# Attention steps in three parts, and column scales applied in the third stage's splits

## The chip, the cores and the metric

The kernel runs on one core of a Trainium2 chip. The metric is the time of one execution in microseconds of the device; the median of three runs is given. TensorE (PE) multiplies, VectorE (DVE) and ScalarE (ACT) do the work between, GpSimd (POOL) very little, and SyncE (SP) issues nearly all DMAs through one queue.

## The reference

```
q_n, k_n = rmsnorm(q, g_q), rmsnorm(k, g_k)            # 4 x 12 heads, 448 x 64
attn = softmax(q_n @ k_n.T / sqrt(64))
x = (attn @ v) laid out as 1792 x 768                  # 4 batches of 448 rows
x = ((x @ w_a) * (x @ w_b)) @ w_out                    # 768 -> 1536 -> 768
h = x @ w_in                                           # 768 -> 2048
g = max(h, 0) + alpha * min(h, 0)                      # alpha: one per column of h
out = g @ w2_out                                       # 2048 -> 768
```

The four weight matrices come as 64-bit floats (the kernel reads them as pairs of 32-bit words), everything else as 32-bit floats.

## The kernel before

The kernel works batch by batch (four batches, b = 0 to 3) and keeps every activation transposed, features on partitions and the 448 rows of the batch along the free dimension. Four stages follow attention for each batch: **a** (the product of the two first matmuls, 24 units of weights of 128 columns), **y** (12 units, two per block of 128 columns), **h** (16 units, with the leaky part behind it) and **o** (24 units, four per block of columns). The order of the stages is written out in the list `stages`: a0 y0 h0 o0 a1 y1 a2 h1 o1 y2 a3 h2 y3 o2 h3 o3.

Each operand of these matmuls is split into two 16-bit halves (a high half by ScalarE, `x[:, 0]`, the rest by VectorE, `x[:, 1]`), and `prod` makes three matmuls of 128x448 of each pair. To stay within 16 bits, weights and activations are scaled by powers of two. For weights the scale is one per column of the result: `w_convert` unpacks a 64-bit unit into 32 bits (ScalarE line 631, VectorE lines 634 and 637) and sums its squares (line 653); `w_scale` adds them over partitions with a small matmul (`total`, names `tot` and `tots`) and makes the scale `sc` and its inverse, kept in `inv`; `w_split` makes the two halves (lines 686 and 687) and stores them in a scratch in HBM, from which the later batches load them. Units are loaded 10, converted 8, summed 6 and split 3 units ahead of their use (`STEPS`). Only the first batch's stages (a0, y0, h0, o0) convert weights.

The inverse scales of stages a, y and o are applied when the result leaves PSUM. Those of stage h are not: the converted weights of stage o are multiplied by them, row block by row block (line 643, `inv["h"]`). Stage h itself takes each result out of PSUM in two steps (`t`, lines 832 and 833) and splits it with one scale `cg` for all blocks into `G[b, f]`. `slot` and `slot32` take tiles from a pool of 35 that all these operands share. In stage o, `finish` scales a result (line 847), transposes it on TensorE (line 854), multiplies it by the product of all scales left, `cum` (line 856, VectorE), and writes it out.

Attention goes in steps. A step m covers two blocks of 128 queries: `scores(m + 1)` on TensorE, `soft(m)` (maximum on VectorE, exponentials `pf` on ScalarE), `probs(m - 1)` (division, two 16-bit halves `p16`, DMA transposes into `pT`), then preparations for later pairs of heads (`prep0` squares, `prep1` inverse roots, `prep2` to `prep4` scaling, halves and transposes of q and k; `vnorm`, `vscale`, `vprep2` for v), and for a finished pair `pv` and `pv_out`, which makes a block of x. The first batch's attention runs alone at the start. The steps of the later batches are put between the units of the stages by `RATE`: 14 steps over the 24 units of a1, for instance. All of this is one program order; a scheduler then sets the final order on each engine, and each engine works through its own in order.

Of the kernel before, what the change touches and what calls it, by code (L numbers as in the profile page):

```python
# [19 lines left out]
def attention_gated_mlps_kernel(  # L20
# [73 lines left out]
    icg = const.tile([128, 1], F32, name="icg")  # L94
    ssv = const.tile([KP, B, NP], F32, name="ssv")
# [365 lines left out]
    def probs(m):  # L461
        if 2 * m < NP * NI:
            probs_f(m)
            return
# [4 lines left out]
        for j in range(2):  # L469
# [13 lines left out]
            )  # L483

# [44 lines left out]
    state = dict(pin=True)  # L529
# [3 lines left out]
    def att_steps():  # L533
# [3 lines left out]
        for m in range(total + 3):  # L537
            if m + 1 < total:
                scores(m + 1)
            if m < total:  # L540
                soft(m)
            if 1 <= m <= total:
                probs(m - 1)
            fin = None
            for n in range(2 * m + 2 if m else 0, 2 * m + 4):
                g, c = divmod(n, NI)
                if n < 2 * total:
                    if g >= NP:
                        if c == 0 and g % NP == 0:
                            vscale(g // NP)  # L550
                        if c == 2:
                            vprep2(g)
                        if c == 3:
                            load_v(g + 2)
                    ahead = (g + 1, g + 2) if g % 2 else ()
                    if c == 0:
                        for x in ahead:
# [13 lines left out]
                    if c == 6 and g + NP < B * NP:  # L571
# [49 lines left out]
    def w_convert(u):  # L621
# [18 lines left out]
        if kind == "o":  # L640
            k = CHAINS["o"][2]
            t3 = t.rearrange("p (k f) -> p k f", f=128)
            nc.vector.tensor_tensor(  # L643
                t3, t3,
                inv["h"][:, part * k:(part + 1) * k].unsqueeze(2).to_broadcast([128, k, 128]),
                op=ALU.mult,
            )
# [13 lines left out]
    def w_scale(u):  # L661
# [10 lines left out]
        for x in us:  # L672
            scales[x] = sc[:, (x - us[0]) // parts:(x - us[0]) // parts + 1]

# [115 lines left out]
    def stage_y(b):  # L790
# [21 lines left out]
        c = cum[:, b:b + 1]  # L812
        nc.gpsimd.tensor_tensor(c, ix[:, b:b + 1], iab[:, b:b + 1], op=ALU.mult)
        nc.gpsimd.tensor_tensor(c, c, iy[:, b:b + 1], op=ALU.mult)
        nc.gpsimd.tensor_tensor(c, c, icg, op=ALU.mult)
        nc.gpsimd.tensor_tensor(c, c, ix[:, b:b + 1], op=ALU.mult)
# [6 lines left out]
    def stage_h(b):  # L823
        for f in range(KF2):
# [6 lines left out]
            t = tmp()  # L831
# [4 lines left out]
            G[b, f] = split(t, cg, f"g{b}_{f}")  # L836
# [3 lines left out]
    def stage_o(b):  # L840
# [3 lines left out]
        def finish(m, ps):  # L844
# [11 lines left out]
            nc.vector.tensor_scalar(ob, po, cum[:PT, b:b + 1], None, op0=ALU.mult)  # L856
# [4 lines left out]

        late = None
# [21 lines left out]
    if True:  # L884
# [20 lines left out]
        while done < NP:  # L905
            g = next(att)
# [15 lines left out]
        for i, st in enumerate(stages):  # L922
# [7 lines left out]
            want, acc = RATE.get(st, 0), 0  # L930
# [35 lines left out]
```

## Time and profile before

| what | value |
|---|---|
| median of 3 runs (lowest, highest) | 1284.11 us (1283.06, 1289.75) |
| profiled execution: time, span | 1286.1 us, 1283.9 us |
| TensorE matmuls, busy | 1177.9 us, 92% |
| VectorE, busy | 709.6 us, 55% |
| ScalarE, busy | 734.5 us, 57% |
| stages a0 to y1 of the page's span | 117.65 to 653.60 us |

The busy share is one over the whole span; the program has a first half in which weights are converted and attention is dense, and a second in which both are thin, so the stretches have to be read one by one. Matmuls are pipelined, and a stretch in which TensorE is always busy runs at full speed only if the granted clock is 1.00 too.

### The profile page before, as it was taken

How to read it: one execution, taken by the hardware profiler on the slowest of the kernel's cores; microseconds unless marked ns; L12 is line 12 of the kernel's file. 1: busy time of each engine (PE TensorE's matmuls, PEld its weight loads, DVE VectorE, ACT ScalarE, POOL GpSimd, SP SyncE). 2: the span in 40 equal slices, each digit the busy share in tenths (PEclk: the TensorE clock that was granted, in tenths of full speed). 3: DMA queues.
4: the chain of work that ended last, by engine and by line, in shares of the span. 5: the costliest groups of instructions: out<-in, count | busy, mean ns of one | idle time of the engine just before them, and what ended most of it. 6: DMA issues, size and time to landing. Idle time of an engine off the chain costs nothing. (4 is left out here: it accounts for less than half of the span.)

```text
span 1283.9 us, 18197 instructions
## 1 busy us (share of the span) xinstructions
PE 1177.9 (92%) x6574; PEld 604.0 (47%) x6574; DVE 709.6 (55%) x1500; ACT 734.5 (57%) x1480; POOL 9.8 (1%) x32
## 2 busy tenths in 40 slices
PE   6897998888888889887999989999999999999998
PEld 3454544444443444443545545555555555555554
DVE  7988788879897857576545166443111351102410
ACT  7999898999886867577554256544222342212310
POOL 1000000000000000000000000000000000000000
PEclk9998998898998999997999999999999999999999
DMA  6548999999989899986865375687533333344343
GB/s 187 157 156 195 299 295 299 268 296 269 285 220 251 238 235 226 206 210 164 204 153 152 115 169 133 153 189 179 150 112 113 121 112 119 94 137 137 104 124 86
DMA packets 324489, 234.66 MB, mean 183 GB/s; under 512 B 190992, under 2 KB 297744, under 8 KB 324400
## 3 DMA queue, kind: packets, MB, share of 16 engines
q1 hardware_dynamic: 324288, 233.43, 68.9%
q8 instruction: 52, 0.85, 0.3%
q0 software_dynamic: 112, 0.07, 0.1%
q14 instruction: 37, 0.30, 0.1%
HBM read 155.79 MB, written 32.24 MB: 146 GB/s over the span
## 5 line engine op out<-in xcount | busy, mean ns | idle before, releaser
L108 PEld LDWEIGHTS <-w 128*128 128x128 f16 x4896 | 480.2, 100 | 488.8 <-issue 55.5
L108 PE MATMUL p<-x,w 128*128 128x448 f16 x1728 | 339.7, 356 | 10.1 <-ACT t L760 6.7
L108 PE MATMUL p<-g,w 128*128 128x448 f16 x1152 | 232.9, 359 | 9.9 <-DVE w L687 6.9
L108 PE MATMUL p<-y,w 128*128 128x448 f16 x1152 | 225.2, 357 | 0.0
L108 PE MATMUL p<-ab,w 128*128 128x448 f16 x864 | 170.8, 359 | 1.9 <-ACT ab L741 1.9
L108 PE MATMUL s<-kT,qT 128*64 128x448 f16 (+1 forms) x588 | 105.5, 408 | 32.4 <-ACT pf L431 24.7
L414 DVE TENSOR_REDUCE nm<-s 128x2 f32<-128x896 f32 x84 | 91.0, 1084 | 36.2 <-PE s L108 35.9
L475 DVE SCALAR_TENSOR_TENSOR p<-pf,ri,p 128x448 f16<-128x448 f32 x126 | 83.2, 680 | 37.9 <-ACT p L474 37.9
L474 ACT ACTIVATE p<-pf,ri 128x448 f16<-128x448 f32 x126 | 79.9, 662 | 31.9 <-DMA pT<-p 23.5
L431 ACT ACTIVATE pf<-s,nm,esc 128x448 f32<-128x448 f32 x126 | 90.2, 720 | 2.9 <-DVE p L475 1.5
L763 DVE SCALAR_TENSOR_TENSOR ab<-p,inv_a,t 128x448 f32<-128x448 f32 x48 | 32.6, 679 | 100.2 <-PE p L108 99.8
L847 ACT ACTIVATE t<-p,inv_o 128x448 f32<-128x448 f32 x24 | 25.6, 1066 | 102.2 <-PE p L108 102.2
L631 ACT ACTIVATE wf<-raw 128x768 f32<-128x768 f32 (+1 forms) x76 | 63.2, 835 | 28.7 <-DMA raw<-in_moe_w_out_dram 8.8
L856 DVE TENSOR_SCALAR ob<-p,cum 112x512 f32<-112x512 f32 x24 | 18.0, 749 | 107.1 <-PE p L854 56.8
L687 DVE SCALAR_TENSOR_TENSOR w<-wf,sc,w 128x768 f16<-128x768 f32 (+1 forms) x76 | 69.8, 927 | 4.0 <-ACT w L686 3.7
L766 ACT ACTIVATE junk<-ab 128x448 bf16<-128x448 f32 x48 | 27.5, 573 | 74.9 <-DVE ab L763 74.1
L833 DVE SCALAR_TENSOR_TENSOR t<-t,al,p 128x448 f32<-128x448 f32 x64 | 43.4, 679 | 47.6 <-ACT t L832 47.6
L637 DVE SCALAR_TENSOR_TENSOR wf<-raw,wf 128x768 int32<-128x768 int32 (+1 forms) x76 | 65.8, 868 | 0.4
L832 ACT ACTIVATE t<-p 128x448 f32<-128x448 f32 x64 | 34.6, 541 | 54.3 <-PE p L108 54.1
L686 ACT ACTIVATE w<-wf,sc 128x768 f16<-128x768 f32 (+1 forms) x76 | 64.5, 862 | 0.3 <-DVE sc L118 0.3
L653 ACT ACTIVATE junk<-wf 128x768 bf16<-128x768 f32 (+1 forms) x76 | 59.0, 776 | 8.5 <-DVE wf L643 2.9
L741 ACT ACTIVATE g<-t,cg 128x448 f16<-128x448 f32 x64 | 42.6, 666 | 34.7 <-DVE t L833 34.6
(131 smaller groups left out, 1003.3 us busy)
## 6 DMA issues: line engine op xcount, KB each, us to landing
w<-sc_a SPq DMA_DIRECT2D x72, 384.0 KB, 3.2
w<-sc_h SPq DMA_DIRECT2D x48, 384.0 KB, 3.1
w<-sc_o SPq DMA_DIRECT2D x72, 256.0 KB, 3.1
w<-sc_y SPq DMA_DIRECT2D x36, 384.0 KB, 3.2
raw<-in_moe_w_in_dram SPq DMA_DIRECT2D x16, 768.0 KB, 7.0
raw<-in_moe_w_out_dram SPq DMA_DIRECT2D x24, 512.0 KB, 5.0
raw<-in_moe_w_a_dram SPq DMA_DIRECT2D x12, 768.0 KB, 7.2
raw<-in_moe_w_b_dram SPq DMA_DIRECT2D x12, 768.0 KB, 6.0
```

The source lines that it names most:

```text
L108: nc.tensor.matmul(out=o, lhsT=a, rhs=b, start=first, stop=last)
L414: nc.vector.tensor_reduce(out=nm, in_=ps[:, :, 0:S], axis=AX.X, op=ALU.max, negate=True)
L431: nc.scalar.activation(out=pf, in_=ps[:, j, 0:S], func=AF.Exp, bias=nm[:, j:j + 1], scale=scale[j], accum_out=su[:, j:j + 1],)
L474: nc.scalar.activation(out=t[:, 0, :, 0:KP], in_=pf, func=AF.Copy, scale=r)
L475: nc.vector.scalar_tensor_tensor(out=t[:, 1, :, 0:KP], in0=pf, scalar=r, in1=t[:, 0, :, 0:KP], op0=ALU.mult, op1=ALU.subtract,)
L631: nc.scalar.activation(out=t, in_=hi.bitcast(F32), func=AF.Prelu, scale=2.0 ** -112, alpha=-(2.0 ** 32))
L637: nc.vector.scalar_tensor_tensor(out=ti, in0=lo, scalar=29, in1=ti, op0=ALU.logical_shift_right, op1=ALU.bitwise_or)
L653: nc.scalar.activation(out=junk(768, size(kind)), in_=t, func=AF.Square, accum_out=sums[0][:, j:j + 1])
L686: nc.scalar.activation(out=w[:, 0], in_=t, func=AF.Copy, scale=s)
L687: nc.vector.scalar_tensor_tensor(out=w[:, 1], in0=t, scalar=s, in1=w[:, 0], op0=ALU.mult, op1=ALU.subtract)
L741: nc.scalar.activation(out=x[:, 0], in_=t, func=AF.Copy, scale=s)
L833: nc.vector.scalar_tensor_tensor(out=t, in0=t, scalar=al[:, f:f + 1], in1=ps, op0=ALU.mult, op1=ALU.add)
```

## The change

Three things are done. Attention steps become three parts each, a `yield` after `soft` and one between the two blocks of `probs`, and the rates count thirds; a few preparations move to other places of a pair. The inverse column scales of stage h are no longer multiplied into stage o's weights; they go, divided by their largest, into the scale with which stage h's results are split (`cgf`, one column per block), and the largest goes into `icg` and with it into `cum`. In the first batch the scales are complete only during stage h, so its early blocks wait as 32-bit tiles until `h_scales` has run. And the output's last scaling moves from VectorE to ScalarE.

```
@@ probs, att_steps
             nc.sync.dma_start_transpose(
                 out=P[g]["pT"][:, :, c, :], in_=t.rearrange("p l i j -> p (l i j)")
             )
+            if j == 0:
+                yield
...
             if m < total:
                 soft(m)
+            yield None
             if 1 <= m <= total:
-                probs(m - 1)
+                for _ in probs(m - 1):
+                    yield None
+            else:
+                yield None
...
-                        if c == 2:
+                        if c == 5:
                             vprep2(g)
-                        if c == 3:
+                        if c == 6:
                             load_v(g + 2)
                     ahead = (g + 1, g + 2) if g % 2 else ()
+                    if g > 1 and g % 2 == 0 and c == 6:
+                        prep0(g + 2)
                     if c == 0:
-                        for x in ahead:
+                        for x in ahead[1 if g > 1 else 0:]:
                             prep0(x)
...
-                    if c == 6 and g + NP < B * NP:
+                    if c == (6 if g % 2 or g < NP else 1) and g + NP < B * NP:
                         vnorm(g // NP + 1, g % NP)
@@ w_convert, w_scale
-        if kind == "o":
-            k = CHAINS["o"][2]
-            t3 = t.rearrange("p (k f) -> p k f", f=128)
-            nc.vector.tensor_tensor(
-                t3, t3,
-                inv["h"][:, part * k:(part + 1) * k].unsqueeze(2).to_broadcast([128, k, 128]),
-                op=ALU.mult,
-            )
...
+        if (kind, n) == ("h", KF2 - 1):
+            h_scales()
+
+    def h_scales():
+
+        mx = sm_p.tile([128, 1], F32, tag="mh", name="mh")
+        ci = sm_p.tile([128, 1], F32, tag="mh", name="ci")
+        nc.vector.tensor_reduce(out=mx, in_=inv["h"], axis=AX.X, op=ALU.max)
+        nc.vector.tensor_scalar(
+            ci.bitcast(I32), mx.bitcast(I32), -1.0, float(254 << 23), op0=ALU.mult, op1=ALU.add
+        )
+        nc.vector.tensor_scalar(cgf, inv["h"], ci, cg, op0=ALU.mult, op1=ALU.mult)
+        nc.gpsimd.tensor_tensor(icg, icg, mx, op=ALU.mult)
+        state["cgf"] = True
@@ stage_h
+        def one(f):
+            t = raw.pop(f)
+            G[b, f] = x = slot(f"g{b}_{f}")
+            nc.scalar.activation(out=x[:, 0], in_=t, func=AF.Copy, scale=cgf[:, f:f + 1])
+            nc.vector.scalar_tensor_tensor(
+                out=x[:, 1], in0=t, scalar=cgf[:, f:f + 1], in1=x[:, 0],
+                op0=ALU.mult, op1=ALU.subtract,
+            )
...
-            t = tmp()
+            raw[f] = t = tmp() if state["cgf"] else slot32(f"g32_{b}_{f}")
...
-            G[b, f] = split(t, cg, f"g{b}_{f}")
+            if state["cgf"]:
+                for x in sorted({f, min(raw)}):
+                    one(x)
+        for x in sorted(raw):
+            one(x)
@@ stage_o, the rates
-            nc.vector.tensor_scalar(ob, po, cum[:PT, b:b + 1], None, op0=ALU.mult)
+            nc.scalar.activation(out=ob, in_=po, func=AF.Copy, scale=cum[:PT, b:b + 1])
...
-            want, acc = RATE.get(st, 0), 0
+            want, acc = 3 * RATE.get(st, 0), 0
```

The five small products that make `cum` move from the end of stage y to the start of stage o, since `icg` is final only then.

What this does to the order on the engines is seen at two places. The first is ScalarE at the end of stage h0, where `g0_15` is the last block's high half, `wf` and `w16` are weights of stage o, and `g32_0_7` is a block that was kept back. Before:

```order
L832 ACTIVATE t_4159<-p_4126 128x448
L653 ACTIVATE junk_4077,ss_3989<-wf_4072 128x512
L474 ACTIVATE p16_0_110<-pf_3910,ri_4106 128x4x112
L474 ACTIVATE p16_1_111<-pf_3912,ri_4106 128x4x112
L344 CAST k16_109<-kr_2992 112x1024
L686 ACTIVATE w16_4189<-wf_3945,sc_4031 128x512
L343 CAST q16_4123<-qr_2991 128x7x64
L631 ACTIVATE wf_4181<-raw_4069 128x512
L741 ACTIVATE g0_15_4162<-t_4159,cg_127 128x448
```

And with the change:

```order
L855 ACTIVATE t_4144<-p_4112 128x448
L841 ACTIVATE g0_6_4147<-g32_0_6_3656,cgf_129 128x448
L428 ACTIVATE nm_4173<-nm_4173,esc_125 128x2
L642 ACTIVATE wf_4196<-raw_4081 128x512
L656 ACTIVATE junk_4138,ss_3973<-wf_4134 128x512
L841 ACTIVATE g0_15_4150<-t_4144,cgf_129 128x448
L841 ACTIVATE g0_7_4153<-g32_0_7_3742,cgf_129 128x448
L841 ACTIVATE g0_8_4156<-g32_0_8_3778,cgf_129 128x448
```

The splits of blocks 6, 7 and 8 now stand around that of block 15, where attention's probabilities and casts stood.

The second is VectorE in the middle of stage a1. `ab32_1_5` is the product that takes a result out of PSUM (line 763 before, 780 with the change), `p16` are probabilities, `qr`, `r`, `t` and `su` belong to attention's preparations and sums. Before:

```order
L467 TENSOR_SCALAR su_5842<-su_5842 128x2
L261 TENSOR_TENSOR t_5950<-r_5949 128x30
L468 RECIPROCAL ri_5939<-su_5842 128x2
L262 SCALAR_TENSOR_TENSOR t_5950<-t_5950,m_5948 128x30
L265 SCALAR_TENSOR_TENSOR r_5949<-t_5950,r_5949 128x30
L383 SCALAR_TENSOR_TENSOR v16_5963<-vr_5439,sx_131,v16_5963 112x8x64
L328 TENSOR_TENSOR qr_5501<-qr_5501,r_5949 128x448
L475 SCALAR_TENSOR_TENSOR p16_2_112<-pf_5845,ri_5939,p16_2_112 128x4x112
L763 SCALAR_TENSOR_TENSOR ab32_1_5_5805<-p_5784,inv_a_138,t_5717 128x448
```

And with the change:

```order
L470 TENSOR_SCALAR su_5804<-su_5804 128x2
L471 RECIPROCAL ri_5899<-su_5804 128x2
L242 TENSOR_REDUCE stat1_115<-sq_6495 128x7
L529 SCALAR_TENSOR_TENSOR x2_1_5766<-x_5741,x2_1_5766 128x448
L384 SCALAR_TENSOR_TENSOR v16_6084<-vr_5486,sx_132,v16_6084 112x8x64
L478 SCALAR_TENSOR_TENSOR p16_2_112<-pf_5807,ri_5899,p16_2_112 128x4x112
L780 SCALAR_TENSOR_TENSOR ab32_1_5_5790<-p_5769,inv_a_139,t_5716 128x448
```

The same product still stands behind the v split and one of the two probability splits; the scaling of q and the small operations on 30 columns are no longer in front of it.

## Rows read from the trace of the kernel before

**Rows 1.** The page, forty equal slices of the span: granted clock in tenths.

```profile
PEclk9998998898998999997999999999999999999999
```

**Rows 2.** Stretches a0 to y1, rest: length, PE, PEld, DVE, ACT, POOL, clock, DMA.

```profile
117.65:231.70 114.05, 101.14 (x559) 51.13 (x557) 95.83 (x196) 100.84 (x199) 0.95 (x1) 0.96 1.03 289
231.70:294.90 63.20, 54.02 (x296) 27.07 (x296) 52.97 (x103) 58.57 (x112) 0.84 (x3) 0.91 1.08 282
294.90:362.85 67.95, 63.49 (x343) 32.28 (x342) 62.29 (x124) 57.88 (x110) 0.00 (x0) 0.95 0.96 275
362.85:466.00 103.15, 84.65 (x465) 39.71 (x464) 89.45 (x198) 80.85 (x173) 0.00 (x0) 0.93 0.92 236
466.00:598.00 132.00, 111.35 (x665) 54.48 (x664) 84.58 (x180) 83.22 (x189) 0.19 (x1) 0.95 0.91 212
598.00:653.60 55.60, 52.78 (x304) 26.26 (x304) 35.16 (x76) 37.33 (x77) 0.00 (x0) 0.96 0.79 182
...
653.60:1284.00 630.40, 619.22 (x3402) 319.78 (x3400) 190.16 (x328) 212.09 (x398) 2.10 (x11) 0.99 0.49 132
```

**Rows 3.** Waits in o0, 362.85 to 466 us: total us, times, longest us.

```profile
ACT wf L631 <- DMA raw<-in_moe_w_out_dram: 7.3, 3, 5.8
PE p L108 <- DVE w L687: 6.9, 5, 2.2
PE p L108 <- ACT w L686: 2.9, 3, 2.0
```

**Rows 4.** Groups by line and form (busy us, mean ns); the last is o0 alone.

```profile
L741 ACT ACTIVATE g<-t,cg 128x448 f16<-128x448 f32 x64 | 42.6, 666 | 34.7 <-DVE t L833 34.6
...
L760 ACT ACTIVATE t<-p,inv_a 128x448 f32<-128x448 f32 x48 | 30.1, 628 | 39.9 <-PE p L108 39.8
...
L856 DVE TENSOR_SCALAR ob<-p,cum 112x512 f32<-112x512 f32 x24 | 18.0, 749 | 107.1 <-PE p L854 56.8 <-DMA w<-sc_o 35.3 <-DMA w<-sc_h 8.8
...
L643 DVE TENSOR_TENSOR wf<-wf,inv_h 128x512 f32<-128x512 f32 x24 | 16.3, 684 | 0.0
...
L643 DVE TENSOR_TENSOR wf<-wf,inv_h 128x512 f32<-128x512 f32 x18 | 12.2, 683 | 0.0
```

**Rows 5.** TensorE in order of time, in o0: start, us, instructions, wait before.

```profile
420.59 4.71 PE L108 MATMUL p<-g,w 128*128 128x448 f16 x24
427.54 4.13 PE L108 MATMUL p<-g,w 128*128 128x448 f16 x12 [2.24 <-DVE w L687]
```

**Rows 6.** ScalarE and SP's queue in order of time, in o0.

```profile
383.93 2.64 SPq L481 DMA_TRANSPOSE pT<-p  x2
...
394.58 0.69 ACT L631 ACTIVATE wf<-raw 128x512 f32<-128x512 f32 x1 [5.81 <-DMA raw<-in_moe_w_out_dram]
```

**Rows 7.** TensorE's waits in a1, 466 to 598 us.

```profile
PE s L108 <- ACT pf L431: 6.4, 3, 3.8
PE p L108 <- ACT t L760: 3.8, 2, 2.8
PE p L108 <- DVE ab L763: 3.1, 1, 3.1
PE tot L108 <- ACT junk L766: 2.0, 1, 2.0
```

**Rows 8.** TensorE and VectorE in order of time, in the middle of a1.

```profile
520.07 6.98 PE L108 MATMUL p<-x,w 128*128 128x448 f16 x36
...
533.86 0.68 DVE L763 SCALAR_TENSOR_TENSOR ab<-p,inv_a,t 128x448 f32<-128x448 f32 x1
```

**Rows 9.** TensorE and VectorE in order of time, h0 and the start of o0.

```profile
332.73 0.59 PE L108 MATMUL tot<-ss,ones 128*128 128x2 f32 x2 [4.46 <-DVE x L524]
...
370.14 2.44 PE L108 MATMUL p<-g,w 128*128 128x448 f16 x12 [1.22 <-DVE w L687]
...
372.13 0.67 DVE L742 SCALAR_TENSOR_TENSOR g<-t,cg,g 128x448 f16<-128x448 f32 x1
```

**Rows 10.** TensorE in order of time, behind the end of a2.

```profile
749.21 0.60 PE L108 MATMUL tot<-ssab,ones 128*128 128x12 f32 x2 [3.66 <-ACT junk L766]
```

More of the change, by code (lines that the diff above doesn't have):

```diff
@@ L94, in attention_gated_mlps_kernel @@
     icg = const.tile([128, 1], F32, name="icg")
+    cgf = const.tile([128, KF2], F32, name="cgf")
     ssv = const.tile([KP, B, NP], F32, name="ssv")
@@ L483, in probs @@
             )
+            if j == 0:
+                yield
     def pv_f(g):
@@ L527, in pv_out @@
         P[g] = None
-    state = dict(pin=True)
+    state = dict(pin=True, cgf=False)
     preps = (prep2, prep3, prep4)
@@ L811, in stage_y @@
         power(t, sy[:, b:b + 1], iy[:, b:b + 1])
[L812 to L816, printed above, removed]
         def one(m):
@@ L823, in stage_h @@
     def stage_h(b):
+        raw = {}
+        def one(f):
[6 more added lines that the diff above has]
+            )
         for f in range(KF2):
@@ L860, in finish @@
             )
+        c = cum[:, b:b + 1]
+        nc.gpsimd.tensor_tensor(c, ix[:, b:b + 1], iab[:, b:b + 1], op=ALU.mult)
+        nc.gpsimd.tensor_tensor(c, c, iy[:, b:b + 1], op=ALU.mult)
+        nc.gpsimd.tensor_tensor(c, c, icg, op=ALU.mult)
+        nc.gpsimd.tensor_tensor(c, c, ix[:, b:b + 1], op=ALU.mult)
         late = None
@@ L905, in attention_gated_mlps_kernel @@
         while done < NP:
-            g = next(att)
+            g = [next(att) for _ in range(3)][-1]
             n += 1
```

## The prediction

> **What bounds the kernel now.** I read the busy time of each engine by stage first [rows 2], beside the granted clock in the page's forty slices [rows 1]. From 653.6 us on TensorE is the bound: it is busy 619.22 of the 630.40 us that are left, at a granted clock of 0.99. Before that it isn't. There the stages a0, y0, h0, o0, a1, y1 last 536 us together, TensorE is idle for 12.9 + 9.2 + 4.5 + 18.5 + 20.7 + 2.8 = 68.6 us of them, and the granted clock is between 0.91 and 0.96. Each stall costs twice: twelve matmuls take 4.13 us after a wait of 2.24 us, where twenty-four took 4.71 us just before [rows 5]. The share (1 - clock) of each stage's length sums to 4.6 + 5.7 + 3.4 + 7.2 + 6.6 + 2.2 = 30 us, an upper estimate of what half speed costs there (1.2 in place of 2.4 GHz).
>
> So what can be won lies in the first half, and two stages hold most of it. In **o0** VectorE is busy 89.45 of 103.15 us; TensorE waits there for converted weights, 6.9 us for their low halves and 2.9 us for their high halves [rows 3]. In **a1** no engine is full (VectorE 64%, ScalarE 63%), and TensorE waits for work that stands late in their queues: 6.4 us for exponentials, 3.8 and 3.1 us for a result to leave PSUM, 2.0 us for a sum of squares [rows 7]. In a0 and y0 the DMA engines are at 1.03 and 1.08 of their time with 289 and 282 GB/s, more than in any later stage.
>
> **The change, part by part.** The terms are summed against the profiled execution (1286.1 us, span 1283.9 us), which lies 2 us above the median of the three runs (1284.11); a gain comes off both alike.
>
> *The multiplication by the column scales (line 643) goes.* 24 instructions of 684 ns are 16.3 us of VectorE, 18 of them and 12.2 us within o0 [rows 4], the others in h0. It stands in the middle of the weight chain: ScalarE unpacks, VectorE shifts, joins and multiplies, ScalarE sums squares, TensorE adds them, VectorE makes the scale, and both split. *The output scaling (line 856) goes to ScalarE.* 24 x 749 ns leave VectorE [rows 4], five of them in o0, 3.7 us. The trace has no ScalarE operation of that form. Nearest is line 760, which reads 128x448 out of PSUM with a scale from a column in 628 ns [rows 4]; 512 columns are a seventh more, so I take 0.69 us, between 0.63 and VectorE's 0.75: 16.6 us of ScalarE in all, 4.1 in o0 for six.
>
> The Trainium skill, "VectorE: DVE Perf Modes", section "The TRN2 errata", gives 172 cycles plus one per element at 1.2 GHz for a ScalarE read of PSUM: an estimate of 570 ns by that page, 13.7 us for 24 in place of 16.6. Line 760 already takes 628 ns for fewer elements, so the row decides and the move costs more than by the page. "ScalarE: Activation LUTs", section "What ACT_TABLE_LOAD costs", adds some 93 ns for a scale taken from a column, which fits the difference.
>
> In o0 VectorE falls from 89.5 to 89.5 - 12.2 - 3.7 = 73.6 us, ScalarE rises from 80.9 to 85.0. The lower bound of the gain is 0: raw weights are late too (line 631 waited 7.3 us for them, [rows 3], once 5.8 us at a stretch, [rows 6]), and ScalarE becomes the fuller engine. The upper bound is both weight waits and all half speed, 9.8 + 7.2 = 17 us. VectorE was 87% busy and is the later of the two engines in 6.9 of the 9.8 us, so the middle is my choice: 7 us of waits and 2 of clock, **9 us**. The next limit is ScalarE, at 85 of the 94 us that are left.
>
> *Stage h of the first batch keeps nine blocks back.* The scales of all sixteen columns are known only when the last group of w2_in has been summed, at the ninth or tenth block. Blocks 0 to 8 stay 32-bit in slots of the pool; blocks 9 to 15 each split one old block as well, and 7 and 8 follow at the end. The instructions are as many as before, but 9 x 0.67 = 6.0 us of ScalarE [rows 4], and about as much of VectorE, move from the first half of h0 to its second. VectorE loses eight multiplications there (5.5 us), ScalarE nothing, and over all of h0 ScalarE was idle only 67.95 - 57.88 = 10 us [rows 2]. What waits behind: o0 multiplies block 7 in its second unit, and block 7 is now last but one in the queues. Before, the last split on VectorE began at 372.13 us, 9.3 us after h0's last matmul, and TensorE met short waits (1.22 us, [rows 9]), since the last blocks come with the fourth unit. Now the second unit, 12 matmuls of 0.19 us further, meets that backlog: at best 4, at worst 10 us more waiting. Some of it isn't lost, as the conversions go on meanwhile and o0's later waits hang on them. Against it stands the wait of 4.46 us in the middle of h0, behind VectorE's split of an attention result [rows 9], for which the first half now has room. I take 3 won and 4 lost, **-1 us**; bounds -10 and +6.
>
> *Attention steps come in thirds.* No instruction is added. In a1, with 14 steps, a step is some 84.6 / 14 = 6 us of VectorE and as much of ScalarE at one place of the order; now scores and exponentials, the first block of probabilities, and the second with the preparations stand at three ticks. Half of the squares, the v split, its load and some norm loads move by a few ticks. The loads pass others in SP's queue, where a pair of probability transposes occupies 2.64 us [rows 6], but as many are issued as before, and v has a whole pair of heads to land. In a1 the evacuation at 533.86 us stood behind a chain of small operations, a v split, a q scaling and a probability split, while its matmuls had ended at 527.05 us [rows 8]; in the new order the q scaling and the small chain are no longer ahead of it. Bounds: +15 (evacuations 6.9, half of the exponentials' 6.4, and most of the clock's 6.6) and -3 (a new order has new waits). The exponentials' 6.4 and the squares' 2.0 lie at the end of a1, where the scores stand as they stood. I take 4 of waits and 1 of clock, **5 us**. In a0 and y0 DMA hides most: **2 us**, bounds -2 and +8. At the ends of y1 and a2 TensorE waits 2.8 us [rows 2] for an attention result's split and 3.66 us for a sum of squares, late in ScalarE's queue [rows 10]; of these and their half speed **3 us**, bounds 0 and 10.
>
> *The rest.* Four small operations for the new scale, once. The product of the scales moves to the start of stage o, on an idle GpSimd, and is needed four units later. After 881 us TensorE covers everything; only the very last scaling is uncovered, and takes about as long on ScalarE.
>
> Sum: 9 - 1 + 5 + 2 + 3 = 18 us. 1286.1 - 18 = 1268.1 for an execution like the profiled one, 1284.1 - 18 = **1266 us** for the median.
>
> **The rivals.**
> *More is won* (B). If the waits for weights and for evacuation are links of one loop, in which a late TensorE makes the conversions late in turn, most of both goes, with the half speed: 17 in o0, 12 in a1, 5 elsewhere, 34 us: 1250 us. For it: 87% of VectorE in o0. Against it: the raw weights late at 394.58 us [rows 6].
> *It does not do what it says* (C). DMA and ScalarE hold the first half: o0 is paced by raw loads behind transposes in SP's queue, a1 by its end. Thirds and multiplication give 0 to 6 us, 1278 to 1290 us with new waits, 1283 in the middle.
> *Slower* (D). ScalarE's late splits in h0. If block 7 comes over 8 us after o0's second unit wants it, 10 us are lost there; ScalarE, filled further by the output scaling, gives o0 nothing back, and a score behind an evacuation costs a1 3 us: 1284 + 10 + 3 = 1297 us. It decides from the point at which ScalarE's queue is more than some 10 us behind TensorE at h0's end; before it was 9.3 us with VectorE as the cause, which is relieved there by 5.5 us.
> The skill's page "PSUM — Partial Sum Buffer", section "Engine vs sequencer instructions", calls ScalarE's and VectorE's queues strictly first in, first out; by that rule block 7 can't overtake, and the evacuation of [rows 8] shows the same.
>
> **How the numbers follow.** The likeliest case (A) is 1256 to 1277, 0.48. B, below 1256, 0.20. C 0.20. D 0.12. A change of 0.5%, 6.4 us, is about what can be told from none: the bounds are 1277.7 and 1290.5. Faster: A, B and 0.04 of C, 0.72. Within: 0.14 of C and 0.03 of D, 0.17. Slower: 0.09 of D and 0.02 of C, 0.11. The range leaves out the far part of B and most of D: 1245 to 1290.
>
> **What would show it.** In the profile of the changed kernel: o0 shorter by 7 to 15 us with VectorE at some 74 us and waits for w of a few us; a wait for g of 4 to 8 us at o0's second unit; a1 shorter by some 5 us with fewer waits for t and ab; everything behind the end of y1 as long as before, 630 us. Wrong: a wait for g over 10 us, or o0 as long as before with waits for raw weights in place of those for w, or more waits for exponentials in a1.

## The result and the profile after

The changed kernel takes **1243.8 us** (median of 6 runs, 1239.7 to 1248.5); the kernel before, beside it, 1287.3 us (6 runs). The ratio is 0.9667, interval [0.9632, 0.9701]: 43 us less. The prediction was 1266 us with a range down to 1245: the sign is right, the gain is more than twice the 18 us forecast, and the time lies 1.2 us below the range. The profiled execution of after (1248.5 us, span 1246.6) is the slowest of its six, so its stages show 37 of the 43 us. One execution of a kernel of the table below, e9_phase_after, took 1730.3 us at a granted clock of 0.654 and has no part in that kernel's ratio.

Stretches a0 to y1 and the rest of the span, after; columns as in [rows 2].

```profile
113.57:223.57 110.00, 100.40 (x573) 51.95 (x572) 99.13 (x198) 103.87 (x204) 0.60 (x1) 0.98 1.09 307
223.57:284.48 60.91, 54.01 (x297) 26.90 (x297) 52.16 (x108) 55.91 (x109) 0.45 (x2) 0.94 1.09 297
284.48:354.33 69.85, 65.83 (x349) 32.83 (x348) 62.91 (x124) 61.79 (x122) 2.59 (x4) 0.93 1.02 286
354.33:448.87 94.54, 80.86 (x463) 38.83 (x461) 76.70 (x173) 82.98 (x178) 0.00 (x0) 0.95 1.06 264
448.87:566.40 117.53, 109.26 (x659) 53.26 (x659) 81.97 (x177) 80.90 (x184) 0.19 (x1) 0.98 1.01 228
566.40:618.55 52.15, 52.15 (x306) 25.73 (x305) 35.08 (x76) 36.77 (x75) 0.00 (x0) 0.98 0.79 186
618.55:1246.60 628.05, 617.65 (x3402) 317.81 (x3400) 176.97 (x310) 224.72 (x417) 2.10 (x11) 1.00 0.49 133
```

Against [rows 2]: a0 -4.0, y0 -2.3, h0 +1.9, o0 -8.6, **a1 -14.5**, y1 -3.5, the rest -2.4, and the start before the first matmul of a0 -4.1 (117.65 to 113.57). In a1 TensorE's idle time falls from 20.7 to 8.3 us and its busy time by 2.1, with the clock from 0.95 to 0.98; in o0 idle falls from 18.5 to 13.7 and busy by 3.8.

TensorE's waits in o0, after (total us, times, longest us), the counterpart of [rows 3]:

```profile
PE s L109 <- DMA kT<-k: 4.0, 2, 2.9
PE p L109 <- ACT w L703: 2.9, 2, 2.1
PE p L109 <- DVE w L704: 2.1, 1, 2.1
...
PE p L109 <- ACT g L841: 1.0, 2, 0.6
PE p L109 <- DVE g L842: 0.2, 1, 0.2
```

Waits for VectorE's weight halves fell from 6.9 to 2.1 us, ScalarE's stayed at 2.9. The late blocks of h0 (`g`) cost 1.2 us.

TensorE's waits in a1, after, against [rows 7]:

```profile
PE tot L109 <- ACT junk L783: 3.0, 1, 3.0
PE s L109 <- ACT pf L432: 2.9, 3, 1.6
PE p L109 <- ACT t L777: 2.4, 2, 1.4
```

The wait for `ab` is gone, exponentials fell from 6.4 to 2.9 us, evacuation (the `t` that takes a result out of PSUM) from 3.8 to 2.4; the wait for the sum of squares rose from 2.0 to 3.0. Two more rows of after: ScalarE's output scaling by group, and the wait in h0 that answers to the one of 4.46 us in [rows 9].

```profile
L883 ACT ACTIVATE ob<-p,cum 112x512 f32<-112x512 f32 x24 | 16.4, 685 | 21.8 <-PE p L881 11.6 <-DMA w<-sc_o 8.3 <-DMA w<-sc_h 1.7
...
320.76 0.59 PE L109 MATMUL tot<-ss,ones 128*128 128x2 f32 x2 [3.67 <-DVE x L529]
```

The output scaling takes 685 ns where 690 was estimated. The Trainium skill, "VectorE: DVE Perf Modes", section "The TRN2 errata", gives by its formula an estimate of some 570 ns for a ScalarE read of 512 columns of PSUM; the measurement decides, the page's figure is a sixth too low for this form. The wait in h0 was forecast to go and stays, at 3.67 us.

### The profile page after: what moved, and what is told of

The parts are those of the page before. It is cut to its first block, busy times and chain, and to the rows that moved or that the text cites. A ratio compares the mean times of both kernels' runs of the same rounds, so it can differ in the third digit from the quotient of the medians.

```text
span 1246.6 us, 18118 instructions
## 1 busy us (share of the span) xinstructions
PE 1170.7 (94%) x6574; PEld 599.9 (48%) x6574; DVE 679.7 (55%) x1455; ACT 745.8 (60%) x1504; POOL 11.6 (1%) x33
## 5 line engine op out<-in xcount | busy, mean ns | idle before, releaser
L109 PE MATMUL p<-x,w 128*128 128x448 f16 x1728 | 335.3, 353 | 2.4 <-ACT t L777 2.4
L109 PE MATMUL p<-g,w 128*128 128x448 f16 x1152 | 229.7, 356 | 6.3 <-ACT w L703 2.9
L856 DVE SCALAR_TENSOR_TENSOR t<-t,al,p 128x448 f32<-128x448 f32 x55 | 37.3, 679 | 95.0 <-ACT t L855 95.0
L855 ACT ACTIVATE t<-p 128x448 f32<-128x448 f32 x55 | 29.7, 540 | 46.8 <-PE p L109 46.4
L841 ACT ACTIVATE g<-t,cgf 128x448 f16<-128x448 f32 x55 | 36.6, 666 | 34.4 <-DVE t L856 34.4
L842 DVE SCALAR_TENSOR_TENSOR g<-t,cgf,g 128x448 f16<-128x448 f32 x55 | 37.6, 683 | 29.6 <-ACT g L841 29.4
```

The lines of the kernel that those rows point to most:

```text
L109: nc.tensor.matmul(out=o, lhsT=a, rhs=b, start=first, stop=last)
L842: nc.vector.scalar_tensor_tensor(out=x[:, 1], in0=t, scalar=cgf[:, f:f + 1], in1=x[:, 0], op0=ALU.mult, op1=ALU.subtract,)
L856: nc.vector.scalar_tensor_tensor(out=t, in0=t, scalar=al[:, f:f + 1], in1=ps, op0=ALU.mult, op1=ALU.add)
```

## The experiments

Theories at the start. (1) *Spreading*: whole steps are bursts at one place of the order, and thirds pay. (2) *VectorE's relief*: the column scales and the output scaling pay, in o0. (3) *The moves* of squares, v splits, v loads and norm loads pay. (4) *Earlier start*: with thirds, a step's scores come two thirds of an interval sooner, and that pays, not the spreading. A rival to all is the prediction's case B, that the waits are *links of one loop*, so that parts pay only together.

All kernels in one table: median, ratio to the kernel before in the same stretch of runs, and from each profiled execution the length of the stages (from a stage's first matmul to the next one's; "start" is what lies ahead of a0, "rest" what lies behind y1).

```
kernel                 us ratio, interval          start     a0    y0    h0     o0     a1    y1   rest
before             1287.3 1                        117.7  114.0  63.2  68.0  103.2  131.9  55.7  630.3
after              1243.8 0.9667 [0.9632, 0.9701]  113.6  110.0  60.9  69.8   94.5  117.5  52.1  628.0
e1_scales          1275.3 0.9932 [0.9906, 0.9958]  117.4  115.7  64.7  66.1   94.9  128.7  55.2  630.3
e2_thirds          1275.2 0.9930 [0.9903, 0.9957]  117.5  109.0  63.8  67.9  108.1  127.6  51.6  628.2
e3_moves           1282.3 0.9976 [0.9961, 0.9991]  112.8  114.2  65.9  67.4  104.8  128.6  56.1  631.5
e5_phase           1276.1 0.9928 [0.9907, 0.9949]  117.1  117.4  61.8  72.9   94.3  123.5  53.3  629.4
e4_whole           1268.9 0.9874 [0.9834, 0.9914]  112.5  116.5  66.3  64.6   97.0  125.6  55.3  630.7
e6_obdve           1247.8 0.9718 [0.9675, 0.9760]  112.0  110.1  58.7  69.2   92.7  117.8  52.6  629.9
e7_nomoves         1261.6 0.9823 [0.9784, 0.9862]  118.8  107.1  65.0  67.0   96.6  125.4  52.4  628.6
e9_phase_after     1259.7 0.9791 [0.9746, 0.9835]  111.5  117.6  61.9  66.9   95.4  122.5  53.5  628.5
e8_two             1264.6 0.9839 [0.9811, 0.9866]  118.7  109.8  65.4  67.1   98.2  127.4  52.1  628.4
e10_vback          1262.8 0.9818 [0.9794, 0.9843]  112.4  109.9  67.5  64.5   99.6  128.4  52.0  628.4
e11_prep0back      1245.4 0.9690 [0.9658, 0.9722]  116.9  107.6  62.5  64.6   93.4  114.6  51.9  629.0
e12_early_thirds   1244.8 0.9680 [0.9651, 0.9710]  111.6  115.5  64.4  63.6   91.4  118.2  55.2  623.6
e13_normback       1262.7 0.9823 [0.9781, 0.9865]  111.2  110.5  63.2  67.9   94.5  132.2  51.6  628.2
e14_splitback      1249.0 0.9708 [0.9667, 0.9749]  111.5  110.9  59.9  67.4   94.6  118.2  51.9  628.7
e15_vback_ob3      1258.4 0.9780 [0.9746, 0.9815]  113.1  108.6  64.9  63.6   98.7  126.9  52.6  629.7
e16_before_ob3     1280.9 0.9951 [0.9929, 0.9973]  117.5  113.4  64.7  63.5  106.4  129.8  55.2  629.7
e17_load_early     1248.1 0.9699 [0.9674, 0.9724]  111.4  110.3  60.7  65.5   96.9  116.1  52.2  628.3
e18_norm_pool      1253.4 0.9734 [0.9711, 0.9756]  116.3  111.3  63.3  65.0   93.5  119.5  51.5  628.6
```

Single runs of one kernel lie some 4 us, at most 8, to either side of its median. A stage's length comes from one execution, so differences under 2 us or so are taken as none; a total is read by its interval.

### One part alone, on the kernel before

**e1_scales** has the column scales and nothing else, **e2_thirds** the yields and threefold rates, **e3_moves** the four edits of places. **e5_phase** leaves steps whole and starts the counter high, so that each comes two thirds of an interval sooner:

```
-            want, acc = RATE.get(st, 0), 0
+            want = RATE.get(st, 0)
+            acc = ticks * 2 // 3 if want else 0
```

> The kernel before with the column scales of stage h moved into its splits (line 643 gone, nine blocks kept back, cum made in stage o), and nothing else: whole attention steps, preparations and the output scaling as before. If most of the 43 us comes from spreading attention (theory 1), this gives what stage o0 alone can give: o0 5 to 9 us shorter, h0 2 to 4 us longer, a0, y0, a1 unchanged within 2 us, 3 to 8 us in all, ratio 0.994 to 0.998. If the relief of VectorE in the weight chain is the main cause (theory 2), 20 us or more, ratio under 0.985.

> The kernel before with attention steps in thirds and the rates counted in thirds, and nothing else: line 643, the preparations' places and the output scaling as before. Theory 1 (spreading): 22 to 32 us, ratio 0.975 to 0.983, with a1 some 12 us shorter, a0 some 6, y1 some 3, and o0 shorter by less than 4. Theory 2 (weight chain): under 10 us, ratio over 0.992, a1 shorter by under 5 us.

> The kernel before with the preparations at their new places only (squares of one pair earlier, v split at c 5, load of v at c 6, some norm loads at c 1). Theory 1: within 4 us of before, ratio 0.997 to 1.003, since as much work stands in as large bursts. Theory 3 (the preparations crowded one step of each pair, and moving them is the gain): 10 us or more, ratio under 0.992, with a1 at least 7 us shorter.

> The kernel before with whole steps, but each a full two thirds of its interval earlier (the counter of every stage starts at two thirds), where the changed kernel has a step's first third. Theory 1 (it is the spreading): within 5 us of before, ratio 0.996 to 1.004, a1 within 4 us. Theory 4 (it is that scores and exponentials start earlier, so that what follows is ready): at least half of what thirds alone give, 12 us or more, ratio under 0.991.

Measured: -0.7%, -0.7%, -0.2% and -0.7%. The first three, which make up the change but for the output scaling, sum to 1.6%, some 21 us; the whole gives 3.3%. So half of the gain exists only in combination. Scales alone bring o0 from 103.2 to 94.9 us, all that o0 gains in the whole change: theory 2 holds for o0, and shows little elsewhere (a1 -3.2). Thirds alone make o0 longer, 108.1 us. TensorE's waits there, in e2_thirds:

```profile
PE p L108 <- DVE w L694: 6.9, 7, 2.7
PE s L108 <- DMA kT<-k: 6.7, 3, 3.5
```

VectorE is as busy in o0 as before (90.8 us against 89.4; the scales are still multiplied in), and keys now come late as well. The moves alone shorten a1 by 3 us. Phase alone gives what thirds alone give, in other stages (o0 -8.9, a1 -8.4, h0 +4.9): the place of a step matters as much as its size. Of the four forecasts only that of e3_moves for theory 1 is met in full; e2_thirds comes near that of theory 2, and e1_scales and e5_phase lie between the two ranges given for them.

### One part undone, from the changed kernel

**e4_whole** makes the steps whole again:

```
-            want, acc = 3 * RATE.get(st, 0), 0
+            want, acc = RATE.get(st, 0), 0
...
-            done += next(att, None) is not None
+            for _ in range(3):
+                done += next(att, None) is not None
```

> The changed kernel, with attention steps whole again (scales, output scaling and preparation moves as changed). Theory 'parts add up': the steps in thirds gave 10 us alone, so this takes some 1254 us (1250 to 1258). Theory 'links of one loop': the parts pay only together, the 13 us by which the whole change beats the sum of its parts go too, and this takes 1262 to 1272 us, with a1 longer than 125 us (117.5 in the changed kernel) and o0 at most 3 us longer. Theory 'the thirds don't matter once VectorE is relieved': 1243 to 1249 us.

1268.9 us, a1 125.6: as the loop theory expected, 2.1% lost where thirds alone had given 0.7%. TensorE's waits in its a1:

```profile
PE s L109 <- ACT pf L432: 6.8, 3, 3.8
PE p L109 <- DVE ab L780: 4.4, 2, 2.7
PE tot L109 <- ACT junk L783: 2.0, 1, 2.0
```

The waits for exponentials are those of before (3.8 at the longest, 6.4 in all, [rows 7]), and the wait for `ab` stands too. Thirds by themselves do not take them away: e13_normback below has thirds and 8.5 us of them.

**e9_phase_after** is e4_whole with e5_phase's counter.

> The changed kernel with whole steps, each two thirds of an interval earlier than its old place. Theory 'spreading' (a step must not stand at one place of the order): as with whole steps at the old place, 1254 us or more. Theory 'earlier start' (what pays is that the scores start at the first tick of their interval): 1243 to 1250 us, with a1 under 121 us. On the kernel before, the same edit gave 9 us alone, and in thirds 10 us.

1259.7 us: 0.8% of the 2.1% come back by an earlier start (a1 122.5, o0 95.4); the intervals [0.9746, 0.9835] and [0.9834, 0.9914] overlap at their very ends. It still lies 1.2% above the changed kernel, which is left to the spreading. The time falls in the range of the spreading; with 0.8% won by the earlier start, theories 1 and 4 both hold in part.

**e6_obdve** puts the output scaling back on VectorE (`nc.vector.tensor_scalar(ob, po, cum[:PT, b:b + 1], None, op0=ALU.mult)`).

> The changed kernel, with the output scaling back on VectorE. If VectorE's 3.7 us in o0 are on the path: 1247 to 1251 us, with o0 97 to 100 us (94.5 in the changed kernel). If ScalarE is the fuller engine in o0 after the change (83.0 of 94.5 us there): 1238 to 1243 us, o0 shorter. If neither is: within 2 us of 1243.8.

1247.8 us, with an interval that overlaps the changed kernel's, and o0 no longer (92.7 us). The total falls in the first case's range and the stage speaks against it: no cost can be told. The 3.7 us of VectorE that the output scaling frees in o0 are worth nothing that is seen here.

**e7_nomoves** undoes all moves; **e8_two** has scales and thirds without moves, on the kernel before (it is e7_nomoves with the output scaling on VectorE).

> The changed kernel without the moves of preparations (first loads, norms, v split at their old blocks). Theory 'parts add up': the moves gave 3 us alone, the start before the first matmul grows from 113.6 to some 117.5 us and this takes 1246 to 1249 us. Theory 'links of one loop': 1250 to 1258 us, with a0, y0 and o0 longer than in the changed kernel by 1.5 us or more each. If the moves only cost something once the steps are in thirds: under 1243 us.

> The kernel before with the column scales and the steps in thirds alone (no preparation moves, output scaling on VectorE). Theory 'links of one loop, any two are worth less than their sum': 1263 to 1270 us. If the two add up (9 + 10 us on 1285): 1265 to 1267 us, no better. If the output scaling on ScalarE matters without the moves: longer than the changed kernel without moves (1261.6 us) by 3 us or more. Below 1260 us would say that the output scaling costs where the moves are missing.

1261.6 us, more than any theory expected: 1.6% lost by undoing what gave 0.2% alone. e8_two takes 1264.6 us: scales and thirds add up (0.7 + 0.7 against 1.6%), and the output scaling is within the error again; the ranges of two theories overlapped here, and the run cannot part them. So the large interaction needs thirds and moves together, and it lies in a1: 127.6 us with thirds alone, 128.6 with moves alone, 125.6 with scales and moves, 127.4 with scales and thirds, 117.5 with all. No kernel has thirds and moves without the scales, so whether those two are enough is not shown.

### Which of the moves

Here the moves are undone piece by piece, in the changed kernel. **e10_vback** takes back v split, v load and norm load, **e14_splitback** v split and v load alone, **e13_normback** the norm loads alone, **e11_prep0back** the squares alone:

```
@@ e10_vback, e14_splitback
-                        if c == 5:
+                        if c == 2:
                             vprep2(g)
-                        if c == 6:
+                        if c == 3:
                             load_v(g + 2)
@@ e10_vback, e13_normback
-                    if c == (6 if g % 2 or g < NP else 1) and g + NP < B * NP:
+                    if c == 6 and g + NP < B * NP:
                         vnorm(g // NP + 1, g % NP)
@@ e11_prep0back
-                    if g > 1 and g % 2 == 0 and c == 6:
-                        prep0(g + 2)
                     if c == 0:
-                        for x in ahead[1 if g > 1 else 0:]:
+                        for x in ahead:
                             prep0(x)
```

> The changed kernel with the v split, the v loads and the norm loads back at their old blocks; half of the squares stay early. Undoing all three moves cost some 18 us (1261.6 us; start +5, a1 +8). If the a1 part comes from the v split and the loads: 1251 to 1257 us, start as in the changed kernel (113.6), a1 122 to 126 us. If it comes from the squares: 1242 to 1247 us. If only all moves together pay: 1257 to 1262 us.

> The changed kernel with the squares of both heads of a pair back at one block; the v split, v loads and norm loads stay moved. If the start before the first matmul hangs on the early squares: start 118 to 119 us (113.6 in the changed kernel). With a1 as in the changed kernel (117 to 119 us): 1248 to 1252 us; if a1's gain hangs on the squares: 1254 to 1260 us.

> The changed kernel with only the norm loads back at their old block. Undoing norm loads, v splits and v loads together took 18 us (1262.8 us). If the norm loads' wait in SyncE's queue is the cause: 1256 to 1263 us, with a wait of 5 to 8 us for the norm load's buffer in that queue in a1. If the v split is the cause: 1243 to 1247 us. If both do part: 1249 to 1255 us.

> The changed kernel with only the v split and the v load back at their old blocks. If the norm loads are the cause: 1243 to 1247 us. If the v split, in one step with the next head's first preparations, is: 1256 to 1263 us. If both do part: 1249 to 1255 us.

e10_vback loses the whole 1.5% (1262.8 us), e11_prep0back nothing that can be told (1245.4; its start is 3 us longer and a0 2.4 us shorter), e14_splitback at most a little (1249.0, intervals overlap), and **e13_normback all of it**: 1262.7 us, with a1 at 132.2 us. Of these forecasts that of e13_normback for the norm loads is met; the time of e14_splitback lies at the edge of the middle range, those of e10_vback and e11_prep0back a little outside the ranges given. What a1 gains hangs on one line, the place of the norm loads of every second pair of heads, six in all: each a load of 112x512 and a square with its sum, 0.63 + 0.19 us of ScalarE.

How it costs so much begins at the start of a1. SP's queue and ScalarE in order of time (start, us, what, and in brackets the idle time before it and its releaser), first e13_normback, whose a1 starts at 447.27 us, then the changed kernel, from 448.87, and the kernel before, from 466.01:

```profile
443.81 0.58 SPq L205 DMA_DIRECT2D kr<-in_k_dram  x1
...
455.71 0.47 SPq L361 DMA_DIRECT2D vn<-in_v_dram  x1
...
460.01 0.63 ACT L369 ACTIVATE sq<-vn 112x512 f32<-112x512 f32 x1 [2.36 <-DMA vn<-in_v_dram]
...
460.77 0.63 ACT L235 ACTIVATE sk<-kr 112x512 f32<-112x512 f32 x1
```

```profile
447.14 0.57 SPq L205 DMA_DIRECT2D kr<-in_k_dram  x1
...
451.79 0.63 ACT L235 ACTIVATE sk<-kr 112x512 f32<-112x512 f32 x1 [2.09 <-DMA kr<-in_k_dram]
```

```profile
480.87 0.63 ACT L368 ACTIVATE sq<-vn 112x512 f32<-112x512 f32 x1
...
481.63 0.63 ACT L234 ACTIVATE sk<-kr 112x512 f32<-112x512 f32 x1
```

In e13_normback the square of a k whose load was issued at 443.81 stands on ScalarE next behind a norm square, whose load left at 455.71, and comes 13.5 us into a1; in the changed kernel it comes 2.9 us into it, and the last norm load ahead of it was issued at 428.09. So attention's preparations enter a1 some 10 us late. All kernels of the table show this. With these norm loads at their old place in SP's queue (before, e1, e2, e5, e7, e8, e10, e13, e15, e16) a norm square comes 8 to 15 us into a1 and a k square close behind it, at 9 to 16 us; in all others the k square comes at 6 us or sooner. This alone does not make a1 short: e3_moves and e4_whole, with whole steps, have the k square at 5.9 and 2.0 us and an a1 of 128.6 and 125.6 us.

TensorE's largest waits in e13_normback's a1 are these:

```profile
PE s L109 <- ACT pf L432: 8.5, 4, 3.7
PE p L109 <- DVE ab L780: 2.8, 2, 2.7
```

How the second comes about can be followed, with VectorE and TensorE in order of time too (other lines between these are left out):

```profile
495.17 0.43 SPq L209 DMA_DIRECT2D qr<-in_q_dram  x1
...
496.12 1.39 SPq L361 DMA_DIRECT2D vn<-in_v_dram  x1
497.61 0.40 SPq L622 DMA_DIRECT2D w<-sc_a  x1
500.73 0.58 ACT L238 ACTIVATE sq<-qr 128x448 f32<-128x448 f32 x1 [4.36 <-DMA qr<-in_q_dram]
502.95 0.62 ACT L369 ACTIVATE sq<-vn 112x512 f32<-112x512 f32 x1
503.69 0.31 SPq L361 DMA_DIRECT2D vn<-in_v_dram  x1
504.09 0.89 SPq L622 DMA_DIRECT2D w<-sc_a  x2
510.27 0.69 DVE L354 TENSOR_TENSOR k<-kr,k 112x512 f16<-112x512 f32 x1
510.98 0.33 SPq L205 DMA_DIRECT2D kr<-in_k_dram  x1
511.41 5.34 SPq L484 DMA_TRANSPOSE pT<-p  x4
513.93 0.63 ACT L235 ACTIVATE sk<-kr 112x512 f32<-112x512 f32 x1 [2.70 <-DMA kr<-in_k_dram]
514.59 0.69 DVE L239 TENSOR_REDUCE stat<-sk 112x8 f32<-112x512 f32 x1 [1.38 <-ACT sk L235]
515.20 0.68 DVE L780 SCALAR_TENSOR_TENSOR ab<-p,inv_a,t 128x448 f32<-128x448 f32 x1
515.92 4.30 PE L109 MATMUL p<-x,w 128*128 128x448 f16 x13 [2.65 <-DVE ab L780]
```

The norm load of 503.69 needs one of two buffers and waits 5.6 us for the square of an earlier one (502.95). That square stands in ScalarE's queue behind a square of q, which waited 4.36 us for its load (issued at 495.17). VectorE waits for that square of q as well (3.77 us), and its preparations come late. SP's queue is past the norm load at 504.98; the next k load (510.98) then waits 6.0 us until VectorE has read the old k (510.27), and four transposes wait behind it. ScalarE then waits 2.70 us for that k, VectorE for ScalarE, and the evacuation behind them on VectorE makes TensorE wait 2.65 us. Three queues, each in its own order, pass one delay round. That the norm load's own wait of 5.6 us is a link of it these rows do not show, and they do not follow the waits for exponentials. In the kernel before, a late k load stands likewise some 10 us ahead of the evacuation of [rows 8], and here it comes ahead of the norm load in the queue:

```profile
518.95 1.10 SPq L204 DMA_DIRECT2D kr<-in_k_dram  x1
...
521.12 0.39 SPq L611 DMA_DIRECT2D w<-sc_a  x1
523.21 0.63 ACT L234 ACTIVATE sk<-kr 112x512 f32<-112x512 f32 x1 [6.05 <-DMA kr<-in_k_dram]
523.87 0.69 DVE L238 TENSOR_REDUCE stat<-sk 112x8 f32<-112x512 f32 x1 [6.43 <-ACT sk L234]
528.32 0.33 SPq L360 DMA_DIRECT2D vn<-in_v_dram  x1
528.76 5.37 SPq L481 DMA_TRANSPOSE pT<-p  x4
```

ScalarE and VectorE stood still for 6 us before that k load landed, and SP's queue from 521.5 to 528.3 before the norm load. In the changed kernel two norm loads leave together in this stretch, with no wait in SP's queue, and four transposes follow; ScalarE still waits 3.29 us for one of the loads:

```profile
492.60 0.93 SPq L361 DMA_DIRECT2D vn<-in_v_dram  x2
...
498.20 0.63 ACT L369 ACTIVATE sq<-vn 112x512 f32<-112x512 f32 x1 [3.29 <-DMA vn<-in_v_dram]
499.16 7.11 SPq L484 DMA_TRANSPOSE pT<-p  x4
```

The Trainium skill, "PSUM — Partial Sum Buffer", section "Engine vs sequencer instructions", calls ScalarE's and VectorE's queues strictly first in, first out; the trace agrees: in the kernel before both stood for 6.05 and 6.43 us behind one load.

Four runs test this reading. **e15_vback_ob3** is e10_vback, **e16_before_ob3** the kernel before, each with `bufs=3` in place of 2 in the pool `ob`, which the norm loads share with the output tiles. **e17_load_early** issues the load at the new place and leaves the square at the old one; **e18_norm_pool** is e13_normback with all norm loads of the later batches issued by GpSimd.

```
@@ e17_load_early
+    VN = {}
...
     def vnorm(b, p):
-        vn = load_vn(b, p)
+        vn = VN.pop((b, p)) if (b, p) in VN else load_vn(b, p)
...
-                    if c == (6 if g % 2 or g < NP else 1) and g + NP < B * NP:
+                    if c == 1 and g % 2 == 0 and g >= NP and g + NP < B * NP:
+                        VN[g // NP + 1, g % NP] = load_vn(g // NP + 1, g % NP)
+                    if c == 6 and g + NP < B * NP:
                         vnorm(g // NP + 1, g % NP)
@@ e18_norm_pool
-        nc.sync.dma_start(
+        (nc.sync if b == 0 else nc.gpsimd).dma_start(
             out=vn, in_=v[b, 2 * p:2 * p + 2].rearrange("h (p i) d -> p h i d", i=KB)
```

> The changed kernel with v split, v loads and norm loads at their old blocks, but three buffers in place of two in the pool that the norm loads share with the output tiles. If what costs the 18 us is the norm load waiting for its buffer in SyncE's queue, with probability transposes and weights behind it: 1243 to 1250 us, the wait gone. If it is the work of split and square on ScalarE and VectorE at those places: 1258 to 1263 us, as with two buffers.

> The kernel before with three buffers in that pool. If the wait in SyncE's queue costs the kernel before too: a1 5 to 10 us shorter, 1275 to 1281 us. If the kernel before has other waits in its place (the moves gave it 3 us only): 1281 to 1287 us.

> The changed kernel with the norm loads of even heads' pairs issued at their new place, but squared at the old one. If the load's place in SyncE's queue costs the 18 us: 1243 to 1250 us. If the square's place in ScalarE's queue does: 1257 to 1264 us. A buffer held longer can cost some of it again: 1250 to 1257 us would leave it open.

> The changed kernel with norm loads and squares at their old place, the norm loads of the second batch on issued from GpSimd's queue in place of SyncE's. If what is behind the waiting load in SyncE's queue makes the cost: 1243 to 1251 us, with probability transposes and loads no longer late and a1 at 117 to 121 us. If the square, or its wait for the load on ScalarE, does: 1257 to 1264 us, a1 126 to 132 us.

A third buffer gives e10_vback back 0.4 of its 1.5% (intervals overlap), a1 126.9 for 128.4 us, and the kernel before 0.5%, with a1 2 us shorter: the wait for the buffer is the smaller part. The time of e15_vback_ob3 lies in the range that its forecast gave to the other cause, the work of split and square; e16_before_ob3 meets the total forecast for a wait that costs, but not its 5 to 10 us in a1. e17_load_early is at 1248.1 us, and its a1 is 116.1 us, the whole of e13_normback's loss, with the square at its old place in the program. Among TensorE's waits in its a1 is none for `ab`:

```profile
PE tot L109 <- ACT junk L787: 3.1, 1, 3.1
PE s L109 <- ACT pf L434: 1.6, 1, 1.6
PE p L109 <- ACT t L781: 1.3, 1, 1.3
```

e18_norm_pool has a1 at 119.5 us, 12.7 of the 14.7 us back, by taking these loads out of SP's queue; its total (1253.4) lies between the two ranges of its forecast and is higher than the a1 would make it, with a longer start and y0 than e17_load_early, and why is not resolved. So it is the load's place in SP's queue that costs, not the square's place in the program.

How it costs is shown in part only, because the scheduler answers each of these edits with another order of the engines. The 19th of the 24 norm squares, 12.7 us into a1 in e13_normback, comes 7.2 us ahead of a1 in e17_load_early and 3.0 us into it in e18_norm_pool; and e13_normback has two norm squares ahead of the first cast of a k in a1, the changed kernel two such casts ahead of the first norm square. What of the 14 us is waiting at run time behind a late load, and what the order made from its new place, no run parts.

### Still more?

**e12_early_thirds** is the changed kernel with e5_phase's counter for its thirds.

> The changed kernel with its thirds each two thirds of their interval earlier (a third of a step's interval is a ninth of some stages). If an earlier start of scores pays on top of the thirds, as it did with whole steps (1268.9 to 1259.7 us): 1236 to 1241 us. If the thirds have already taken what there was: 1241 to 1248 us. If earlier exponentials now stand before evacuations: over 1248 us.

1244.8 us: the thirds have taken what an earlier start gives. Stages change places (a0 +5.5, h0 -6.2, o0 -3.1, the rest -4.4) with no gain. Of all kernels tried none beats the changed one.

## Why the prediction was wrong

**o0, 9 us: right.** 8.6 us measured, 4.8 of idle time and 3.8 of matmul time for the forecast 7 and 2. VectorE fell to 76.7 us there (73.6 forecast), and e1_scales shows the cause by itself. The forecast counted the output scaling in; e6_obdve shows no part of it.

**h0 and the start of o0, -1 us: right in sum, wrong in its working.** h0 is 1.9 us longer. VectorE was to lose eight multiplications there (5.5 us); by [rows 4] it is six, 24 less the 18 of o0, some 4.1 us. The 4 to 10 us of waiting for block 7 at o0's second unit came to 1.2, and the wait of 4.46 us in h0 that was to go stayed at 3.67. Neither rival D's price nor the gain set against it arose.

**a1, 5 us: the step that failed.** It measured 14.5, just inside the stated bound of 15. The text read [rows 8] as a queue of operations ahead of the evacuation, and said of the loads that "as many are issued as before, and v has a whole pair of heads to land", which priced their places at nothing. e13_normback and e17_load_early price the place of the norm loads alone at some 14 us of a1 in the changed kernel. The engines that looked loaded in front of that evacuation had stood idle for 6 us before, for a late load; the wait of SP's queue (6.9 us of it for one norm load's buffer) was not read, nor that the k square at a1's start came 15.6 us into the stage, next behind a norm square. How much of the 14 us is waiting and how much another order stays open. The second error was to leave the exponentials' 6.4 us at a1's end "where the scores stand as they stood": 3.5 of them went, and came back in e4_whole and in e13_normback.

**a0 and y0, 2 us, "DMA hides most": wrong.** They gave 6.3, and the start 4.1, which had no term. The DMA engines did what was asked of them: 307 GB/s in a0 where 289 had been taken for its limit [rows 2]. Thirds alone give a0 5 us. The start's part goes with the early squares: 111 to 114 us in all kernels that have them but e18_norm_pool (116.3), 117 to 119 in those that don't, e11_prep0back among them; a0 gives some of it back, and the total doesn't show it.

**The ends of y1 and a2, 3 us, and the rest, 0:** 3.5 us in y1 and 2.4 behind it. y1 has no idle time left.

**The rivals.** Case B had the mechanism, one loop in which lateness returns, with 34 us, but put half of it into o0; o0 was won by a plain relief of VectorE, and the loop was in a1 and, as far as the rows show it, ran through SP's queue, which the case did not name. That the moves pay 1.3% more with the other parts than alone (1.6% undone in e7_nomoves, 0.2% alone) is shown, and e8_two and e4_whole that it takes the thirds. Why is not: in e4_whole and e13_normback, each with one of the two undone, the waits for exponentials (6.8 and 8.5 us) and for `ab` (4.4 and 2.8 us) both stand. That the half speed counts double is borne out only in part: of the 31 us that the six stages lost, TensorE's idle time gave 26.1 and its busy time 4.9 (467.4 to 462.5 us, with 15 matmuls more in them). The share (1 - clock) of their lengths, an upper estimate, falls from 30 to 2.2 + 3.7 + 4.9 + 4.7 + 2.4 + 1.0 = 19 us.

## What to carry to other kernels

Where engines work through their queues in order, look at the DMA issuer's queue as at any other engine: ask for each load when its buffer comes free, what frees it, and what stands behind it, above all when the load looks small and early enough. Before a late operation is put down to the work just ahead of it, look for an idle time of that engine further up, and follow its releaser back. A table of single effects doesn't sum when two edits work on one loop; undoing one from the whole shows what it is worth there. Where a scheduler sets the order, look at the order it made before a loss is put down to the operation that was moved.

## What the runs showed of the hardware

Six loads of 112x512, each with 0.82 us of work behind it, moved the total by 19 us (1243.8 to 1262.7) by their place in the program and so in one queue. A transfer issued at 495.17 us in e13_normback kept ScalarE waiting until 500.73, over 5 us, with the DMA engines at 1.04 of their time in that stretch. And a0's DMA, at 1.03 of the engines' time and 289 GB/s before, carried 307 GB/s after, at 1.09: a busy share of one did not mean that no more could be moved.
